# Tensor work of the attention units regrouped, four output buffers, a Sigmoid pass for the first gates, and a new order of the first stage

## The chip, the cores and the metric

One core of one Trainium2 chip runs the whole program. The metric is the device time of that core in microseconds. TensorE (PE) does the matrix products, VectorE (DVE), ScalarE (ACT) and GpSimd (POOL) work on its results, SyncE (SP) issues the transfers. All times of traces are counted from the start of the span of one profiled execution.

## The reference

Three parts follow each other. All data are float32.

```python
# linear attention with a gate, q, k, v, f_logit of shape (4, 8, 768, 48)
f = 1 / (1 + exp(-f_logit))
for t in range(S):
    state = f[t, :, None] * state + outer(k[t], v[t])     # 48 x 48 for each of 4 batches and 8 heads
    y[t] = q[t] @ state
# gated layer on 3072 tokens of width 384
xn = x / sqrt(mean(x * x) + 1e-6) * rms_g
x = (silu(xn @ w_gate) * (xn @ w_val)) @ w_out            # 384 -> 1536 -> 384
# second layer
out = relu(x @ w_in) ** 2 @ w_out2                        # 384 -> 2048 -> 384
```

## The kernel before, in words

The sequence of 768 is cut into 6 chunks of 128 steps. A *unit* is one chunk of one batch: 24 units in the order of chunks, units 0 to 3 being chunk 0. Four units are a *group* of 512 tokens, so there are six groups.

**A unit.** Two heads lie in each of four pairs, 64 partitions a head. The gate goes through `gate` (from unit 4 on, `sig` on both halves of `fr`: tanh, then an affine pass) or `gate_part` (units 0 to 3, `r` and `f` apart). VectorE runs a scan backwards (`scan_b`) and one forwards (`scan_a`), multiplies k and q by the results (`mul_k`, `mul_q`). TensorE then makes `scores` (L317, products of k and q of half height, two side by side), VectorE masks them (`mask_part`), TensorE transposes the keys (`ktrans`, L337) and ScalarE copies them out of PSUM (`kcopy`). `attend` (L352) adds two things in one PSUM bank: for chunks after the first the *inter-chunk products* q times state (L358, four, each 128 columns wide and 96 elements moving), and the *intra-chunk products* of masked scores and v (L371, sixteen, each 64 columns wide and 48 elements moving). `kv` (L378) makes the products of transposed keys and v that `state_add` adds to the state; the last chunk has neither `ktrans` nor `kv`. `norm`, `power`, `norm2` normalise the rows, `xtrans` transposes them, and `xhigh`, `xlow` split them into two fp32r parts (xh on ScalarE, L439, xl on VectorE, L446). Each of the float32 products is run by TensorE as two instructions, so four inter-chunk products are eight rows of the trace.

**The projections.** Every float32 weight and input is used as a high and a low part, and `mm3` makes three fp32r products of 512 (L555 to L557) for one. A step f of the gated layer has a piece G, a piece V and a piece O of nine such products each; between them stand Silu (si, L682), the product with V (vs, L687, on VectorE) and the split of the result (hh on ScalarE, L690, hl on VectorE, L692).

**The order of the first stage.** `first()` goes through the list `FIRST`, written out by hand. Every word is a piece and a number: l* are loads, gr and gf the gates, sb, sa, mk, mq, sc, ma, mb, kt, kc, y, kv, st, no, pw, nr, xt, xh, xl the parts of a unit in the order above (en keeps the last gate product, de decays the state), wl loads a pair of weights, ws, wb, wc make float32 of it, wh and wz split it, G, si, V, vs, hh, hl, O are a step of group 0. The list holds units 0 to 7, the 18 weight pairs of the gated layer and the twelve steps of group 0. Each engine takes its own pieces in this order and waits for what a piece needs. VectorE's pieces are sb, sa, mk, mq, ma, mb, xl, vs, hl, wb, wc, wz and st from unit 4 on.

**Phase 1.** For groups 1 to 5 `phase1` (L705) runs G, V and the O of the step before; behind each of the three stands a slot, and `plan_unit` (L582) puts the parts of units 8 to 23 into slots relative to the unit's own slot s, nine slots a unit. The slot's side parts (loads, ScalarE and VectorE) come ahead of the step's own ScalarE and VectorE work, its tail parts (TensorE) behind:

```python
(-9, (load_unit,)), (-3, (gate,)), (-2, (scan_b, keep_end)), (-1, (scan_a, mul_k)), (0, (mul_q, decay)),
(1, (masked,)), (2, (kcopy,)), (3, (norm, power)), (4, (state_add, norm2)), (6, (xhigh, xlow)),
...
((0, scores), (1, ktrans), (2, attend), (3, kv), (5, xtrans))
```

At a group's end `evac_x3` (L616) copies the three accumulators on ScalarE and stores them. The weights of the second layer are converted in phase 1 too.

**Phase 2.** For each group 16 steps: `project` (nine products of 512, written h), Relu on ScalarE (L751), square on VectorE (L752), split (L753, L754), and `seg_o2` (L729, twelve products of 384, written o) for the step before. At the last step of a group `seg_o2` copies four accumulators to SBUF, on ScalarE (L740) and VectorE (L738) in turn, into tiles of the tag qk, of which there are two, and stores each (L741). The next group's first `seg_o2` writes the same PSUM banks.

Of the kernel before, what the change touches and what calls it, by code (L numbers as in the profile page):

```python
# [8 lines left out]
F32 = mybir.dt.float32  # L9
# [3 lines left out]
AF = mybir.ActivationFunctionType  # L13
# [3 lines left out]
P = 128  # L17
B, H, S, D = 4, 8, 768, 48
# [3 lines left out]
DM = H * D  # L22
# [7 lines left out]


FIRST = """
lr0 lf0 lq0 lf1 lr1 gr0 lk0 lf3 gf0 sb0 sa0 mq0 lk1 lq1 gr1 lr2 lr3 gf1 mk0 lf2 sb1 sc0 gf3 lv0 wl0 mk1 gr2
mb0 kt0 sa1 kc0 lk2 gf2 lk3 mq1 sb2 lv1 sc1 lq2 lq3 kt1 ma0 kv0 en2 gr3 lv2 ma1 y0 ld4 mb1 st0 sa2 y1 kc1 no0
sb3 pw0 wl1 mk3 nr0 xt0 sa3 ws0 mq2 no1 lv3 ld5 mk2 xh0 pw1 nr1 wb0 sc2 kv1 xl0 xt1 st1 mq3 sc3 kt2 xh1 ma2
gr4 mb2 xl1 y2 mb3 ma3 ws1 wc0 sb4 y3 no2 kc2 wl2 no3 pw2 mk4 pw3 wb1 nr2 kv2 wh0 xt2 nr3 wc1 xt3 st2 sa4 wl3
xh3 xh2 mq4 wz0 sc4 wh1 xl3 ws2 xl2 kt3 G0 wz1 ws3 wb2 gr5 V0 wc2 wb3 wl4 kt4 si0 wc3 de4 G1 mb4 wh2 wl5 ma4
wh3 y4 wz2 ws4 vs0 wz3 kc4 wb4 hh0 kv4 V1 kc3 wc4 ws5 si1 hl0 kv3 no4 st4 G2 vs1 pw4 wb5 wl6 nr4 st3 xt4 wc5
O0 xh4 hh1 sb5 wl7 xl4 en5 V2 wh4 hl1 wh5 wz4 en4 si2 O1 ld6 wz5 ws6 vs2 ws7 wb6 G3 hh2 wc6 V3 hl2 wl8 wh6 wb7
wc7 si3 O2 mk5 wl9 wh7 gr6 wz6 wz7 G4 sa5 mq5 ws8 vs3 sb6 hh3 V4 si4 ws9 wb8 wc8 sc5 kt5 en0 G5 wb9 wh8 wl10  # L40
kc5 wz8 vs4 ma5 V5 hh4 hl3 hl4 wc9 si5 mk6 ws10 O3 de5 mb5 wl11 wh9 wb10 y5 en1 wc10 kv5 de6 wz9 wl12 O4 st5
ws11 kt6 vs5 G6 wb11 wh10 wz10 hh5 no5 wc11 ws12 V6 pw5 hl5 wl13 nr5 wb12 kc6 si6 xt5 O5 xh5 vs6 ld7 sa6 hh6
wh11 G7 xl5 hl6 wz11 mq6 V7 ws13 wc12 sc6 si7 wh12 wl14 wb13 gr7 wc13 O6 ma6 wl15 wz12 en3 G8 ws14 mb6 wh13
sb7 vs7 kv6 de7 y6 wz13 si8 wb14 hh7 hl7 ws15 G9 en6 wc14 wb15 O7 wh14 wl16 si9 wc15 wl17 no6 wh15 sa7 pw6 V8
nr6 wz15 xt6 mk7 G10 ld8 xh6 mq7 en7 st6 vs8 sc7 wz14 V9 hh8 xl6 ws16 ws17 mb7 ma7 hl8 y7 vs9 wb16 kt7 no7 O8
wc16 kc7 si10 pw7 wb17 hh9 V10 wh16 wc17 nr7 wz16 wh17 kv7 xt7 xh7 wz17 G11 vs10 xl7 V11 hl9 si11 st7 O9 hh10
vs11 hh11 hl10 O10 hl11 O11
"""


# [139 lines left out]
def tile_linear_attention_moe(  # L190
# [11 lines left out]
    nc = tc.nc  # L202
# [3 lines left out]
    def pool(name, **kw):  # L206
        return main.enter_context(tc.tile_pool(name=name, **kw))
# [6 lines left out]
    ap_ = pool("attn", bufs=2)  # L214
# [17 lines left out]
    state = [cp.tile([P, NPAIR, 2 * D], F32, name=f"state{b}") for b in range(B)]  # L232
# [21 lines left out]
    U = {}  # L254
# [23 lines left out]
    def sig(x):  # L278
        nc.scalar.activation(x, x, AF.Tanh, scale=0.5)
        nc.scalar.activation(x, x, AF.Identity, bias=half, scale=0.5)  # L280
# [2 lines left out]
        sig(U[u]["fr"].rearrange("p x a t -> p (x a) t")[:, :, 1:])  # L283

    def gate_part(n, u):
        sig(U[u][n][:, :, 1:])

    def scan_b(u):
        r = U[u]["r"]
# [24 lines left out]
    def banks(u):  # L314
        return ("pa", "pb", "pc") if u >= UG or u % 2 == 0 else ("acc0", "acc1", "acc2")
# [36 lines left out]
    def attend(u):  # L352
        c, b = units[u]
        y = ps.tile([P, DM], F32, tag=banks(u)[0], name=f"y{u}")
        first = True
        if c:
            for p in range(NPAIR):
                nc.tensor.matmul(  # L358
                    y[:, p * 2 * D:(p + 1) * 2 * D], U[u]["q"][:, p], state[b][:, p],
                    start=first, stop=False, skip_group_check=True,  # L360
                )
                first = False
        sub = [first, first]
        for hf in range(2):
            sm = U[u]["sm", hf]
            for j in range(4):
                h = 2 * j + hf
                hs = slice(h * D, (h + 1) * D)
                for i in range(2):
                    o = slice(64 * i, 64 * i + 64)  # L370
                    nc.tensor.matmul(  # L371
                        y[o, hs], sm[:, j, o], U[u]["v"][:, hs],
                        start=sub[i], stop=True, skip_group_check=True,
                    )
                    sub[i] = False
        U[u]["y"] = y
# [177 lines left out]
    def mm3(o, lh, ll, rh, rl, first, last):  # L554
        nc.tensor.matmul(o, lh, rh, start=first, stop=False)  # L555
        nc.tensor.matmul(o, lh, rl, start=False, stop=False)  # L556
        nc.tensor.matmul(o, ll, rh, start=False, stop=last)  # L557
# [21 lines left out]
    def at(where, s, fn):  # L579
        where.setdefault(max(s, NG), []).append(fn)  # L580

    def plan_unit(u, s):  # L582
        for k, fns in (
            (-9, (load_unit,)), (-3, (gate,)), (-2, (scan_b, keep_end)), (-1, (scan_a, mul_k)), (0, (mul_q, decay)),
            (1, (masked,)), (2, (kcopy,)), (3, (norm, power)), (4, (state_add, norm2)), (6, (xhigh, xlow)),
        ):
            for fn in fns:
                if fn is not load_unit or u > 2 * UG:
                    at(side, s + k, lambda fn=fn: fn(u))
        for k, fn in ((0, scores), (1, ktrans), (2, attend), (3, kv), (5, xtrans)):  # L590
            at(tail, s + k, lambda fn=fn: fn(u))

    NG = 3 * F1
    for gi in range(1, NU - 1):
        for j in range(UG):
            plan_unit((gi + 1) * UG + j, gi * NG + (3 if gi == 1 and j == 0 else (1, 10, 19, 28)[j]))
# [58 lines left out]
    def piece(kind, i):  # L655
        if kind in ("lr", "lk", "lf", "lq", "lv"):
            load_part(kind[1], i)
        elif kind in ("gr", "gf"):
            gate(i) if i >= UG else gate_part(kind[1], i)
        elif kind in ("ma", "mb"):  # L660
            mask_part(i, kind == "mb")
        elif kind in unit_piece:
            unit_piece[kind](i)
        elif kind in pair_piece:
            pair_piece[kind](w1_order[i])
        else:
            step_piece(kind, 0, i)

    unit_piece = dict(
        ld=load_unit, sb=scan_b, en=keep_end, sa=scan_a, mk=mul_k, mq=mul_q, sc=scores, kt=ktrans, kc=kcopy,  # L670
        y=attend, kv=kv, de=decay, st=state_add, no=norm, pw=power, nr=norm2, xt=xtrans, xh=xhigh, xl=xlow,
    )
    pair_piece = dict(wl=wload, ws=wscale, wb=wbits_low, wc=wbits_sign, wh=whigh, wz=wlow)
# [55 lines left out]
    def seg_o2(gi, f, hid, acc):  # L729
        wh, wl = W["b", f]  # L730
        for j in range(UG):
            cs = slice(j * C, (j + 1) * C)
            mm3(acc[j], hid[0][:, cs], hid[1][:, cs], wh, wl, f == 0, f == F2 - 1)
            if f == F2 - 1:
                c, b = units[gi * UG + j]
                o = ap_.tile([P, DM], F32, tag="qk", name=f"o_{gi}_{j}")
                if j % 2:
                    nc.vector.tensor_copy(o, acc[j])  # L738
                else:
                    nc.scalar.copy(o, acc[j])  # L740
                nc.sync.dma_start(out[b * S + c * C:b * S + (c + 1) * C, :], o)  # L741

    def phase2():
        for gi in range(NU):
            xh, xl = X[NU + gi]
            for f in range(F2):
                hps = ps.tile([P, N], F32, tag=("g", "vv")[f % 2], name=f"h2_{gi}_{f}")
                project(hps, ("a", f), xh, xl)
                sg = hp.tile([P, N], F32, tag="sg", name=f"r_{gi}_{f}")
                hh, hl = hidden(f"2_{gi}_{f}")  # L750
                nc.scalar.activation(sg, hps, AF.Relu)  # L751
                nc.vector.tensor_mul(sg, hps, sg)  # L752
                nc.scalar.copy(hh, sg)  # L753
                nc.vector.tensor_sub(hl, sg, hh.bitcast(F32))  # L754
                if gi + 1 < NU and f == 4:
                    load_x3(gi + 1)
                if gi + 1 < NU and f == 9:
                    parts.extend(split_x3(gi + 1))
                if parts:
                    parts.pop(0)()  # L760
                if pend:
                    pend.pop()()
                if f == 0:
                    acc = [ps.tile([P, DM], F32, tag=("acc0", "acc1", "acc2", "pa")[j], name=f"o2_{gi}_{j}") for j in range(UG)]
                pend.append(lambda gi=gi, f=f, hid=(hh, hl), acc=acc: seg_o2(gi, f, hid, acc))
        pend.pop()()
# [73 lines left out]
```

## Time and profile before

| | |
|---|---|
| median of 3 runs | 999.11 us (998.51 to 999.23) |
| the profiled execution, its own time | 998.11 us |
| its span | 996.3 us |
| mean granted clock of TensorE | 0.989 of full speed |
| TensorE busy | 967.3 us, 5757 products |
| VectorE busy | 506.6 us |
| ScalarE busy | 423.6 us |

How to read it: an engine's busy time is the time in which one of its instructions ran; products are pipelined, so a product's own duration (0.39 us for 512 columns) is longer than the distance to the next start. That distance is the cost. The granted clock is given as a share of 2.4 GHz; TensorE has a second level at 1.2 GHz, and a stretch with a mean between 0.5 and 1.0 has run at both. "Idle before, releaser" names what ended an idle time.

### The profile page before, as it was taken

The page shows a single profiled execution, that of the slowest core. Times are in us where ns is not written, and L with a number is a line of the kernel's source. Part 1 is how long each engine was busy: PE and PEld are TensorE (multiplying, and loading weights), DVE is VectorE, ACT ScalarE, POOL GpSimd, SP SyncE. Part 2 cuts the span into 40 slices and gives each one's busy share as a digit, 9 for nine tenths or more (in the row PEclk, how much of TensorE's full clock was granted, in tenths as well). Part 3 has the DMA queues.
Part 4 walks back from the last instruction along what each step waited for, and adds up shares of the span by engine and source line. Part 5 has one row for each costly group of instructions (what it writes and reads, how often), then busy time and mean ns, then how long its engine had stood idle before and what let it go on. Part 6 is the DMA issues. An engine that isn't in the chain of part 4 may idle for free.

```text
span 996.3 us, 14143 instructions
## 1 busy us (share of the span) xinstructions
PE 967.3 (97%) x5757; PEld 822.6 (83%) x5757; DVE 506.6 (51%) x777; ACT 423.6 (43%) x810; POOL 19.6 (2%) x42
## 2 busy tenths in 40 slices
PE   6799999999999999999999999999999999999996
PEld 4677878888888888888888889989989899899895
DVE  7999965555555666565522233333334334333332
ACT  6866645455455545454431233333323323333222
POOL 1000000000000000000000000000000000000000
PEclk7899999999999999999999999999999999999999
DMA  9455433334333433243036530010010100100001
GB/s 342 151 177 181 175 146 114 115 115 156 135 133 135 168 136 115 83 177 115 32 127 222 190 128 1 1 64 1 16 48 1 64 1 1 64 1 1 32 1 35
DMA packets 34744, 97.03 MB, mean 97 GB/s; under 512 B 4208, under 2 KB 10352, under 8 KB 34672
## 3 DMA queue, kind: packets, MB, share of 16 engines
q1 hardware_dynamic: 34672, 96.06, 27.3%
q8 instruction: 47, 0.77, 0.3%
q14 instruction: 25, 0.20, 0.1%
HBM read 74.02 MB, written 22.02 MB: 96 GB/s over the span
## 4 chain that ended last, share of the span: by engine, by line
PE 88%; DVE 6%; DMA 3%; ACT 1%; issue 1%; SPq 0%; DVEq 0%; ACTq 0%
PE o L555 7%; PE o L557 6%; PE h L556 6%; PE h L557 6%; PE o L556 6%; PE h L555 6%; PE acc L555 5%; PE v L555 5%; PE acc L557 5%; PE acc L556 5%; PE v L557 5%; PE v L556 5%; PE g L555 4%; PE g L557 4%; PE g L556 4%; PE y L371 2%
## 5 line engine op out<-in xcount | busy, mean ns | idle before, releaser
L752 DVE TENSOR_TENSOR r<-h,r 128x512 f32<-128x512 f32 x96 | 66.3, 691 | 181.9 <-ACT r L751 181.9
L751 ACT ACTIVATE r<-h 128x512 f32<-128x512 f32 x96 | 57.4, 598 | 190.1 <-PE h L557 190.1
L555 PE MATMUL o<-wh_a,hh 128*128 128x384 f32 x384 | 130.0, 339 | 0.6
L557 PE MATMUL o<-wh_a,hl 128*128 128x384 f32 x384 | 129.7, 338 | 0.1
L556 PE MATMUL o<-wl_a,hh 128*128 128x384 f32 x384 | 129.0, 336 | 0.0
L557 PE MATMUL h<-xh,wl_a 128*128 128x512 f32 x288 | 113.9, 396 | 0.0
L556 PE MATMUL h<-xl,wh_a 128*128 128x512 f32 x288 | 113.7, 395 | 0.0
L555 PE MATMUL h<-xh,wh_a 128*128 128x512 f32 x288 | 112.0, 389 | 0.0
L687 DVE TENSOR_TENSOR sg<-v,sg 128x512 f32<-128x512 f32 x72 | 49.7, 690 | 119.7 <-PE v L557 117.5
L754 DVE TENSOR_TENSOR hl<-r,hh 128x512 fp32r<-128x512 f32 x96 | 66.4, 692 | 65.9 <-PE o L557 56.9
L753 ACT CAST hh<-r 128x512 fp32r<-128x512 f32 x96 | 59.6, 621 | 74.2 <-DVE r L752 74.2
L682 ACT ACTIVATE sg<-g 128x512 f32<-128x512 f32 x72 | 43.0, 597 | 110.1 <-PE g L557 107.8
L690 ACT CAST hh<-sg 128x512 fp32r<-128x512 f32 x72 | 44.4, 616 | 89.9 <-DVE sg L687 87.3
L555 PEld LDWEIGHTS o<-wh_a,hh 128*128 128x128 f32 x384 | 72.1, 188 | 7.0 <-DVE o L738 2.2
L556 PEld LDWEIGHTS o<-wl_a,hh 128*128 128x128 f32 x384 | 72.1, 188 | 4.1
L557 PEld LDWEIGHTS o<-wh_a,hl 128*128 128x128 f32 x384 | 72.0, 188 | 0.4 <-DVE hl L754 0.4
L557 PEld LDWEIGHTS h<-xh,wl_a 128*128 128x128 f32 x288 | 54.0, 187 | 11.6
L556 PEld LDWEIGHTS h<-xl,wh_a 128*128 128x128 f32 x288 | 54.0, 187 | 9.1
L555 PEld LDWEIGHTS h<-xh,wh_a 128*128 128x128 f32 x288 | 54.1, 188 | 8.7
L692 DVE TENSOR_TENSOR hl<-sg,hh 128x512 fp32r<-128x512 f32 x72 | 49.0, 682 | 14.3 <-ACT hh L690 13.7
L555 PE MATMUL v<-xh,wh_g 128*128 128x512 f32 x108 | 44.1, 408 | 1.5 <-DVE sg L687 1.5
L555 PE MATMUL v<-xh,wh_v 128*128 128x512 f32 x108 | 44.2, 409 | 0.7 <-DVE sg L687 0.7
(127 smaller groups left out, 1832.1 us busy)
## 6 DMA issues: line engine op xcount, KB each, us to landing
raw<-in_w_dram SPq DMA_DIRECT2D x34, 768.0 KB, 4.4
w2d<-ws_a SPq DMA_DIRECT2D x32, 384.0 KB, 2.5
ff<-in_ff_dram SPq DMA_DIRECT2D x20, 516.0 KB, 4.6
qk<-in_qk_dram SPq DMA_DIRECT2D x20, 512.0 KB, 5.7
wh_a<-w2d SPq DMA_DIRECT2D x16, 384.0 KB, 3.1
wl_a<-w2d SPq DMA_DIRECT2D x16, 384.0 KB, 3.9
v<-in_vp_dram SPq DMA_DIRECT2D x24, 192.0 KB, 5.7
x3d<-x3o SPq DMA_DIRECT2D x18, 256.0 KB, 2.1
```

Source lines behind the costliest of these rows:

```text
L371: nc.tensor.matmul(y[o, hs], sm[:, j, o], U[u]["v"][:, hs], start=sub[i], stop=True, skip_group_check=True,)
L555: nc.tensor.matmul(o, lh, rh, start=first, stop=False)
L556: nc.tensor.matmul(o, lh, rl, start=False, stop=False)
L557: nc.tensor.matmul(o, ll, rh, start=False, stop=last)
L682: nc.scalar.activation(dd["s", f], dd["g", f], AF.Silu)
L687: nc.vector.tensor_mul(dd["s", f], dd["v", f], dd["s", f])
L690: nc.scalar.copy(dd["h", f][0], dd["s", f])
L692: nc.vector.tensor_sub(dd["h", f][1], dd["s", f], dd["h", f][0].bitcast(F32))
L751: nc.scalar.activation(sg, hps, AF.Relu)
L752: nc.vector.tensor_mul(sg, hps, sg)
L753: nc.scalar.copy(hh, sg)
L754: nc.vector.tensor_sub(hl, sg, hh.bitcast(F32))
```

## The change

1. `attend`: each inter-chunk product is made in two of 64 columns, in the two halves of the array, in turn.
2. `plan_unit`: the key transposes move from slot 1 to slot 0, ahead of the scores; their copy from slot 2 to slot 1; k v moves from slot 3 to slot 2, behind the intra-chunk products.
3. `seg_o2`: the copies of accumulators 2 and 3 go to tiles of the tag ff, so a group has four output buffers.
4. `gate_part`: one Sigmoid pass for r and f of units 0 to 3, where tanh and an affine pass stood.
5. `FIRST`: the same 385 pieces in another order.

```diff
--- before.py
+++ after.py
@@ -30,21 +30,21 @@
 
 
 FIRST = """
-lr0 lf0 lq0 lf1 lr1 gr0 lk0 lf3 gf0 sb0 sa0 mq0 lk1 lq1 gr1 lr2 lr3 gf1 mk0 lf2 sb1 sc0 gf3 lv0 wl0 mk1 gr2
-mb0 kt0 sa1 kc0 lk2 gf2 lk3 mq1 sb2 lv1 sc1 lq2 lq3 kt1 ma0 kv0 en2 gr3 lv2 ma1 y0 ld4 mb1 st0 sa2 y1 kc1 no0
-sb3 pw0 wl1 mk3 nr0 xt0 sa3 ws0 mq2 no1 lv3 ld5 mk2 xh0 pw1 nr1 wb0 sc2 kv1 xl0 xt1 st1 mq3 sc3 kt2 xh1 ma2
-gr4 mb2 xl1 y2 mb3 ma3 ws1 wc0 sb4 y3 no2 kc2 wl2 no3 pw2 mk4 pw3 wb1 nr2 kv2 wh0 xt2 nr3 wc1 xt3 st2 sa4 wl3
-xh3 xh2 mq4 wz0 sc4 wh1 xl3 ws2 xl2 kt3 G0 wz1 ws3 wb2 gr5 V0 wc2 wb3 wl4 kt4 si0 wc3 de4 G1 mb4 wh2 wl5 ma4
-wh3 y4 wz2 ws4 vs0 wz3 kc4 wb4 hh0 kv4 V1 kc3 wc4 ws5 si1 hl0 kv3 no4 st4 G2 vs1 pw4 wb5 wl6 nr4 st3 xt4 wc5
-O0 xh4 hh1 sb5 wl7 xl4 en5 V2 wh4 hl1 wh5 wz4 en4 si2 O1 ld6 wz5 ws6 vs2 ws7 wb6 G3 hh2 wc6 V3 hl2 wl8 wh6 wb7
-wc7 si3 O2 mk5 wl9 wh7 gr6 wz6 wz7 G4 sa5 mq5 ws8 vs3 sb6 hh3 V4 si4 ws9 wb8 wc8 sc5 kt5 en0 G5 wb9 wh8 wl10
-kc5 wz8 vs4 ma5 V5 hh4 hl3 hl4 wc9 si5 mk6 ws10 O3 de5 mb5 wl11 wh9 wb10 y5 en1 wc10 kv5 de6 wz9 wl12 O4 st5
-ws11 kt6 vs5 G6 wb11 wh10 wz10 hh5 no5 wc11 ws12 V6 pw5 hl5 wl13 nr5 wb12 kc6 si6 xt5 O5 xh5 vs6 ld7 sa6 hh6
-wh11 G7 xl5 hl6 wz11 mq6 V7 ws13 wc12 sc6 si7 wh12 wl14 wb13 gr7 wc13 O6 ma6 wl15 wz12 en3 G8 ws14 mb6 wh13
-sb7 vs7 kv6 de7 y6 wz13 si8 wb14 hh7 hl7 ws15 G9 en6 wc14 wb15 O7 wh14 wl16 si9 wc15 wl17 no6 wh15 sa7 pw6 V8
-nr6 wz15 xt6 mk7 G10 ld8 xh6 mq7 en7 st6 vs8 sc7 wz14 V9 hh8 xl6 ws16 ws17 mb7 ma7 hl8 y7 vs9 wb16 kt7 no7 O8
-wc16 kc7 si10 pw7 wb17 hh9 V10 wh16 wc17 nr7 wz16 wh17 kv7 xt7 xh7 wz17 G11 vs10 xl7 V11 hl9 si11 st7 O9 hh10
-vs11 hh11 hl10 O10 hl11 O11
+lr0 lf0 lk0 lq0 lr1 gr0 sb0 lf1 lk1 gf0 wl0 mk0 gr1 sa0 gf1 mq0 kt0 lv0 lr2 sb1 sc0 lq1 mk1 lr3 ws0 ma0 lf2
+sa1 lk3 gr2 lv1 mb0 lq2 wb0 lf3 kc0 lk2 kt1 mq1 kv0 st0 lq3 wc0 gf2 ld4 sb2 kc1 sc1 sa2 mq2 gr3 wh0 y0 no0 pw0
+wl1 gf3 mb1 kv1 ma1 mk2 y1 st1 lv2 nr0 lv3 wz0 ld5 no1 pw1 xt0 sc2 sb3 mk3 sa3 mq3 xh0 nr1 xt1 sc3 gr4 wl2 xl0
+kt2 mb2 ma2 ma3 y2 ws1 xh1 kc2 mb3 y3 wb1 kv2 no2 pw2 no3 pw3 en3 xl1 nr2 xt2 sb4 sa4 mk4 nr3 xt3 st2 xh3 mq4
+wc1 wl3 xh2 sc4 ws2 xl3 xl2 kt3 wb2 ma4 kc3 G0 wh1 de4 en1 V0 wz1 en4 wc2 ws3 kt4 mb4 si0 G1 wb3 wh2 vs0 wz2
+kv3 en2 wl4 wc3 gr5 sb5 ws4 wl5 V1 kc4 kv4 wh3 wb4 wc4 wl6 y4 si1 hh0 wz3 G2 wh4 no4 pw4 vs1 V2 mk5 hh1 wz4
+ws5 hl1 st3 ld6 hl0 wb5 wc5 ws6 kt5 kc5 nr4 wb6 O0 si2 vs2 wl7 O1 wc6 sa5 hh2 xt4 wh5 en0 G3 wl8 xh4 mq5 wh6
+wz5 ws7 xl4 V3 si3 wz6 st4 sc5 ws8 wb7 vs3 wc7 wl9 hh3 G4 V4 wb8 wh7 gr6 hl2 O2 wc8 hl3 si4 ma5 O3 wl10 wh8
+wz7 wz8 vs4 ws9 wb9 hh4 ws10 mb5 de5 G5 wc9 wh9 en5 y5 wb10 wc10 wl11 wl12 si5 V5 wz9 hl4 wh10 vs5 no5 pw5
+ws11 wz10 G6 wb11 kv5 ld7 nr5 hh5 xt5 xh5 O4 hl5 O5 wc11 si6 xl5 wl13 ws12 sb6 en6 de6 mk6 kt6 st5 wh11 gr7 V6
+G7 si7 kc6 wb12 wc12 wl14 sa6 mq6 vs6 wz11 sb7 wh12 sc6 hh6 V7 ws13 wz12 G8 hl6 O6 wb13 ws14 vs7 hh7 V8 si8
+wc13 wl15 mb6 de7 ma6 hl7 wb14 wc14 wh13 wh14 y6 no6 wl16 O7 sa7 wz13 pw6 kv6 vs8 mq7 hh8 st6 ws15 G9 mk7 nr6
+wz14 kt7 sc7 wb15 kc7 si9 xt6 ws16 V9 wc15 wl17 hl8 O8 xh6 wh15 xl6 wz15 vs9 wb16 hh9 hl9 G10 V10 ws17 wc16
+wh16 mb7 si10 wb17 O9 ma7 y7 wc17 wh17 en7 wz16 G11 vs10 wz17 hh10 hl10 no7 V11 ld8 pw7 si11 vs11 kv7 st7 nr7
+xt7 O10 hh11 hl11 O11 xh7 xl7
 """
 
 
@@ -283,7 +283,8 @@
         sig(U[u]["fr"].rearrange("p x a t -> p (x a) t")[:, :, 1:])
 
     def gate_part(n, u):
-        sig(U[u][n][:, :, 1:])
+        x = U[u][n][:, :, 1:]
+        nc.scalar.activation(x, x, AF.Sigmoid)
 
     def scan_b(u):
         r = U[u]["r"]
@@ -352,15 +353,16 @@
     def attend(u):
         c, b = units[u]
         y = ps.tile([P, DM], F32, tag=banks(u)[0], name=f"y{u}")
-        first = True
+        sub = [True, True]
         if c:
             for p in range(NPAIR):
-                nc.tensor.matmul(
-                    y[:, p * 2 * D:(p + 1) * 2 * D], U[u]["q"][:, p], state[b][:, p],
-                    start=first, stop=False, skip_group_check=True,
-                )
-                first = False
-        sub = [first, first]
+                for i in range(2):
+                    o = slice(64 * i, 64 * i + 64)
+                    nc.tensor.matmul(
+                        y[o, p * 2 * D:(p + 1) * 2 * D], U[u]["q"][:, p, o], state[b][:, p],
+                        start=sub[i], stop=False, skip_group_check=True,
+                    )
+                    sub[i] = False
         for hf in range(2):
             sm = U[u]["sm", hf]
             for j in range(4):
@@ -582,12 +584,12 @@
     def plan_unit(u, s):
         for k, fns in (
             (-9, (load_unit,)), (-3, (gate,)), (-2, (scan_b, keep_end)), (-1, (scan_a, mul_k)), (0, (mul_q, decay)),
-            (1, (masked,)), (2, (kcopy,)), (3, (norm, power)), (4, (state_add, norm2)), (6, (xhigh, xlow)),
+            (1, (kcopy, masked)), (3, (norm, power)), (4, (state_add, norm2)), (6, (xhigh, xlow)),
         ):
             for fn in fns:
                 if fn is not load_unit or u > 2 * UG:
                     at(side, s + k, lambda fn=fn: fn(u))
-        for k, fn in ((0, scores), (1, ktrans), (2, attend), (3, kv), (5, xtrans)):
+        for k, fn in ((0, ktrans), (0, scores), (2, attend), (2, kv), (5, xtrans)):
             at(tail, s + k, lambda fn=fn: fn(u))
 
     NG = 3 * F1
@@ -733,7 +735,7 @@
             mm3(acc[j], hid[0][:, cs], hid[1][:, cs], wh, wl, f == 0, f == F2 - 1)
             if f == F2 - 1:
                 c, b = units[gi * UG + j]
-                o = ap_.tile([P, DM], F32, tag="qk", name=f"o_{gi}_{j}")
+                o = ap_.tile([P, DM], F32, tag=("qk", "ff")[j // 2], name=f"o_{gi}_{j}")
                 if j % 2:
                     nc.vector.tensor_copy(o, acc[j])
                 else:
```

## Rows read from the trace of the kernel before

**Rows 1.** The page: span, and busy time of each engine.

```profile
span 996.3 us, 14143 instructions
...
PE 967.3 (97%) x5757; PEld 822.6 (83%) x5757; DVE 506.6 (51%) x777; ACT 423.6 (43%) x810; POOL 19.6 (2%) x42
```

**Rows 2.** Stretches: length; busy and instructions of PE, PEld, DVE, ACT, POOL; clock; DMA.

```profile
6.50:79.00 72.50, 56.76 (x509) 46.22 (x509) 70.03 (x106) 54.34 (x107) 3.97 (x5) 0.88 0.62 221
146.00:500.00 354.00, 353.87 (x2398) 289.54 (x2397) 208.56 (x329) 171.91 (x356) 8.76 (x16) 1.00 0.34 122
```

**Rows 3.** Timeline of PE around one unit: start, duration, instruction.

```profile
191.59 0.48 PE L555 MATMUL g<-xh,wh_o 128*128 128x512 f32 x1
191.91 0.39 PE L556 MATMUL g<-xl,wh_o 128*128 128x512 f32 x1
...
193.50 0.39 PE L557 MATMUL g<-xh,wl_o 128*128 128x512 f32 x1
193.73 1.02 PE L358 MATMUL y<-state,qk 128*128 128x96 f32 x8
194.69 1.14 PE L371 MATMUL y<-v,sm 128*64 128x48 f32 x32
...
196.09 0.40 PE L556 MATMUL v<-xl,wh_v 128*128 128x512 f32 x1
...
197.71 0.40 PE L557 MATMUL v<-xh,wl_v 128*128 128x512 f32 x1
198.04 0.56 PE L386 MATMUL kv<-v,ktok 128*48 128x48 f32 x16
...
198.87 0.40 PE L556 MATMUL acc<-hl,wh_o 128*128 128x512 f32 x1
```

**Rows 4.** Timeline of PE, unit 5 of the first stage.

```profile
83.04 0.39 PE L557 MATMUL acc<-hh,wl_v 128*128 128x512 f32 x1
...
85.19 0.53 PE L386 MATMUL kv<-v,ktok 128*48 128x48 f32 x16
...
85.99 0.40 PE L556 MATMUL acc<-hl,wh_o 128*128 128x512 f32 x1
```

**Rows 5.** Timeline of PEld (weight loads), the same unit as rows 3.

```profile
187.96 0.97 PEld L323 LDWEIGHTS sc<-qk 64*128 64x128 f32 x16 [0.35 <-issue]
...
194.68 1.01 PEld L371 LDWEIGHTS y<-v,sm 128*64 128x64 f32 x32
```

**Rows 6.** Waits: who waited for whom, us in total, times, longest.

```profile
ACT o L740 <- DMA out_dram<-o: 13.2, 6, 3.3
...
PEld o L555 <- DVE o L738: 2.2, 5, 0.5
```

**Rows 7.** Timeline of all engines, the end of phase 2.

```profile
986.89 0.34 PE L557 MATMUL o<-wh_a,hl 128*128 128x384 f32 x1
...
989.92 0.56 DVE L738 COPY o<-o 128x384 f32<-128x384 f32 x1 [3.14 <-DMA out_dram<-o]
```

**Rows 8.** The chain that ended last, the end of phase 2: start, us, what.

```profile
986.80 3.00 DMA out_dram<-o
```

**Rows 9.** Timeline of the first stage and the start of phase 1.

```profile
0.81 1.28 ACT L279 ACT_TABLE_LOAD   x1 [0.81 <-PEq L829]
...
5.70 0.72 ACT L280 ACTIVATE r<-r,half 128x512 f32<-128x512 f32 x1
...
6.52 1.23 DVE L290 TENSOR_TENSOR_SCAN r<-r,floor 128x516 f32<-128x516 f32 x1 [6.52 <-ACT r L280]
...
79.09 0.47 PE L555 MATMUL v<-xh,wh_v 128*128 128x512 f32 x1 [0.72 <-DVE sg L687]
...
135.76 1.95 ACT L619 COPY x3o<-acc 128x512 f32<-128x512 f32 x3 [2.10 <-PE acc L557]
...
144.94 1.16 PE L323 MATMUL sc<-qk 64*128 64x128 f32 x16 [1.74 <-DVE qk L304]
```

**Rows 10.** Groups by line: busy us, mean ns of one, idle before.

```profile
L439 ACT ACTIVATE xh<-xtp,gT 128x128 fp32r<-128x128 f32 x72 | 20.9, 368 | 2.8 <-PE xtp L428 2.7
```

## The prediction

> **What bounds the kernel now.** I read the page first: TensorE is busy for 967 of 996.3 us, VectorE for half of that [rows 1]. So two questions decide: what fills TensorE, and where its 29 us of idle lie. The view by stretches answers the second. From 6.5 to 79 us VectorE is the bound: busy 70.03 of 72.5 us, while TensorE idles 15.7 us, at a granted clock of 0.88, so part of it at the lower level, 1.2 GHz [rows 2]. From 146 to 500 us TensorE is busy 353.87 of 354 us and VectorE 208.56 [rows 2]. There every microsecond taken off TensorE comes off the end. The last idle stretch is the end of phase 2, after the last product.
>
> The timeline of TensorE around one unit (unit 10, 188 to 199 us) shows what a unit costs beside the projections. Seven projection products lie between 191.91 and 193.50 us, 0.227 us each [rows 3]. After the key transposes the first product takes 0.32 us to the next start (191.59 to 191.91), 0.09 too long. The attention visit runs from the start of the product ahead of it (193.50) to the second one behind it (196.09): 2.59 us, of it 0.96 (193.73 to 194.69) the eight instructions of the inter-chunk products, including the change to the half-width ones. The k v visit, measured in the same way, is 1.16 us (197.71 to 198.87), with 0.33 from the product ahead to its own start instead of 0.227: changing to half-width products and back costs time each time.
>
> **k v behind the intra-chunk products.** Two separate visits take 2.59 + 1.16 us and contain two ordinary steps more than a joint one: 3.75 - 2 x 0.227 = 3.30 us. In the first stage there is a joint one already, from 83.04 to 85.99 us, 2.95 us [rows 4]. Gain 0.35 us less reading error: I take 0.34 for each of units 8 to 19 (the last chunk has no k v): 12 x 0.34 = **4.1 us**. Nothing takes its place: the copy of the transposed keys still has one whole step of nine products and the next projection between the transposes and k v; if ScalarE were late by more than that, TensorE would wait at k v for it.
>
> **Key transposes ahead of the scores.** The separate visit ends in the 0.09 us of above; joined to the scores, that end falls together with the change that the scores cost anyway. 0.09 for eleven units: **1.0 us** (unit 8 stands in a wait, below). Bounds 0 and 0.2 each.
>
> **Inter-chunk products split.** Eight full-width instructions become sixteen of 64 columns, moving 96 elements. No row shows this shape. Bounds: the half-width products of the intra-chunk part move 48 elements at 1.01/32 = 31.6 ns of weight loads each; the scores, two half-arrays side by side, move 128 at 0.97/16 = 60.6 ns [rows 5]. In proportion to what moves, 96 of 128 gives 45 ns, 0.73 us for sixteen; the change to half width (0.10) now stands ahead of them and not behind. 0.73 + 0.10 against 0.96: gain 0.13. The ends: 16 x 31.6 ns would gain 0.35, 16 x 60.6 ns would lose 0.11. I take 0.13, since the scores are nearest in size: 16 units x 0.13 = **2.1 us** (-1.8 to +5.6). Against it speaks the Trainium skill, "TensorEngine Tiling (Array Packing)", section Instruction Overhead: about 60 cycles for each matmul, so tiling doesn't pay from a dimension that is already small. By it eight more instructions would cost some 0.2 us a unit, an estimate from that page, and the sum would be 5 us higher; no row here shows that price, and the 31.6 ns products bear it out only in part.
>
> **Four output buffers.** In phase 2 the third and fourth copy of each group wait for a transfer: ScalarE 13.2 us in six waits [rows 6]. TensorE feels it at the five inner group borders, where a weight load waits 2.2 us in total for the last copy [rows 6]. With a buffer for each copy these end: **2.0 us**. At the end the last product starts at 986.89 and runs 0.34 us, but the last copy starts only at 989.92 [rows 7]; it could start at 987.27, 2.65 us earlier. A transfer there takes 3.00 us with two in flight [rows 8]. With four in flight the gain lies between 0.7 (the second pair moves wholly behind the first: lands at 992.8 and not at 993.5) and 2.65. I take **2.2 us**, nearer to the second end, since the two transfers of that row are in flight together and still take no longer than 3.00.
>
> **The first stage.** VectorE starts at 6.52 us, when ScalarE has done tanh and a 0.72 us affine pass on the first gate [rows 9]. One Sigmoid pass drops the 0.72, and seven more behind it: VectorE starts 0.7 earlier. A table load takes 1.28 us on ScalarE [rows 9], and the program has two; a third one by this change would cost between 0 and 1.28; I take 0, since it would fall where VectorE has queued work. The Trainium skill, "ScalarE: Activation LUTs", section Table sets: the hidden batching unit, lists tanh in sigmoid's set, so by it none is added; no row here shows Sigmoid. VectorE's idle of 72.5 - 70.03 = 2.5 us to 79 us is mostly waiting for ScalarE early on; I take 0.5 back. The same pieces stand in both written orders, so VectorE's total is fixed and only places move. The piece that decided before is V5, the last one for which TensorE waited, at 79.09 us, for the gated product of step 4 [rows 9]. I count 105 VectorE instructions in the order up to that product (the window up to 79 us has 106 [rows 2], 0.66 us each); the new order has 103, and one O piece and one unit's attention fewer behind it. G8 comes next: 136 instructions instead of 139 ahead of its weights, but fourteen steps of nine products instead of thirteen behind: about -2 and +2 us. So I give the order 0.3. Weight load wl0 now stands ahead of the second unit's loads on SP's queue and delays them; sb1 and the weights' work are there to cover it, else VectorE idles, see the rivals.
>
> One step is worse: xh7 and xl7 now stand behind O11. ScalarE's three copies after O11 ran from 135.76 for 1.95 us [rows 9]; behind them comes xh7 (368 ns a piece [rows 10]), then xl7, about as long (an estimate from that row), ahead of the first G of group 1: TensorE idles some 1.3 us. But 1.74 us of waiting for unit 8's scores (at 144.94 us [rows 9]) follow anyway. Unit 8's gate is put back by three pieces of xh7, some 0.9 us, and the transposes now fill 0.4 of that wait: net +0.4. First stage: -0.7 - 0.5 - 0.3 + 0.4 = **-1.1 us**.
>
> **Sum:** 4.1 + 1.0 + 2.1 + 2.0 + 2.2 + 1.1 = 12.5 us. The profiled execution took 998.11 us, so 985.6; the median shown is 999.11, 1.0 above it. Forecast 986.6 us.
>
> **Rivals.**
> 1. *The split costs time.* At 60.6 ns or more per half-width product the term is -1.8 instead of +2.1: 990.5 us. For it: twice the instructions. Against it: 31.6 ns for the existing half-width ones. The skill page above is this rival's rule; by its price the time would be 991.9, an estimate. Chance 0.13.
> 2. *The first stage slips.* The late loads of units 1 to 3, a third table load and the wait for xl7 add up on VectorE's start of the dense part: 4 to 5 us more, 991. For it: only 2.5 us of VectorE idle to win back, more to lose. Chance 0.17.
> 3. *VectorE runs dry ahead of G0: slower.* The new order does the weights of V0 behind 23 VectorE instructions, before behind 46: the work that filled the waits for four units' normalisation is spent early. Each microsecond that VectorE then idles comes at the end one for one, and TensorE, idling too, starts the dense part at 1.2 GHz. It decides from 10.5 us of extra idle (no change) and is slower from 14.5. Price with 15 us: 1001.6. Against it: ScalarE has 5.8 us less to do there. Chance 0.10 (0.04 within 0.2%, 0.06 beyond).
> 4. *The first stage gains more:* all 2.5 us of VectorE idle return: 984.5. Chance 0.05.
> That the joint visits don't come about is no rival of its own: the order of the slots fixes them; only the first stage's own k v pieces stay apart for units 5 to 7.
>
> **Numbers.** Forecast 0.55. Range: from 980.5 (the better first stage with the split at 31.6 ns, 3.5 us better, less a little) to 993 (rivals 1 and 2 half joined, or the last pair of transfers at its bad end). A measurement of this kernel can tell 0.2%, 2 us, from no change. Faster: all but rival 3, 0.90; same 0.04; slower 0.06.
>
> **What would show it.** In the profile after: the unit visit in TensorE's timeline with k v right behind the intra-chunk products, without a visit of its own, and sixteen inter-chunk instructions in 0.7 to 0.8 us. A unit of chunks 2 to 4 then takes 0.56 us less from its scores to the next unit's. No wait of ScalarE or VectorE copies for the output transfer. VectorE's first scan at 5.8 us. An idle of TensorE of about 1.3 us ahead of the first G of group 1. It is wrong if VectorE shows more than 5 us of idle up to 79 us, if TensorE waits for transposed keys at k v, or if the sixteen instructions take over 0.96 us.

## The result, and the profile after

The changed kernel takes 983.81 us (median of four, 983.71 to 984.16), the kernel before in the same session 998.81: a ratio of 0.9852, 95% interval 0.9835 to 0.9869. Forecast were 986.6 us and a gain of 12.5; the gain is 15.0 us by the medians and 14.3 by the two profiled spans. The numbers of the source lines moved by one to three: L358 is L361 now, L371 L373, L555 to L557 are L557 to L559.

The page of the changed kernel, span and busy time [rows 1]:

```profile
span 982.0 us, 14472 instructions
...
PE 959.8 (98%) x5917; PEld 818.6 (83%) x5917; DVE 506.6 (52%) x777; ACT 417.4 (43%) x802; POOL 17.8 (2%) x42
```

TensorE has 160 products more (twenty units with eight instructions more each) and is busy 7.5 us less; VectorE's work is the same to a tenth; ScalarE, without the eight affine passes, is busy 6.2 us less. The stretches, in the same columns and between the same times as [rows 2] (VectorE now starts at 5.44 us, ahead of the first):

```profile
6.50:79.00 72.50, 62.36 (x553) 50.76 (x554) 70.40 (x108) 52.17 (x106) 3.19 (x5) 0.84 0.62 225
...
146.00:500.00 354.00, 354.00 (x2563) 291.59 (x2563) 212.12 (x335) 173.74 (x362) 9.22 (x16) 1.00 0.35 124
```

VectorE still bounds the first and TensorE the second. Up to 79 us TensorE now idles 10.1 us and not 15.7, but at a granted clock of 0.84 and not 0.88, so part of the longer busy time is work at the lower level. VectorE has done 108 instructions and not 106.

TensorE's timeline of unit 10, the same unit as [rows 3] (start, duration, instruction):

```profile
185.38 0.39 PE L559 MATMUL v<-xh,wl_g 128*128 128x512 f32 x1
185.60 0.60 PE L343 MATMUL ktp<-ident,qk 128*128 128x128 f32 x4
186.13 1.16 PE L324 MATMUL sc<-qk 64*128 64x128 f32 x16
187.22 0.50 PE L557 MATMUL acc<-hh,wh_v 128*128 128x512 f32 x1
...
191.22 0.39 PE L559 MATMUL g<-xh,wl_o 128*128 128x512 f32 x1
191.53 0.88 PE L361 MATMUL y<-state,qk 128*64 128x96 f32 x16
192.24 1.09 PE L373 MATMUL y<-v,sm 128*64 128x48 f32 x32
193.16 0.53 PE L388 MATMUL kv<-v,ktok 128*48 128x48 f32 x16
193.62 0.50 PE L557 MATMUL v<-xh,wh_v 128*128 128x512 f32 x1
193.96 0.39 PE L558 MATMUL v<-xl,wh_v 128*128 128x512 f32 x1
...
208.93 1.16 PE L324 MATMUL sc<-qk 64*128 64x128 f32 x16
```

The scores of units 10 and 11 in the kernel before, for the distance between them:

```profile
187.96 1.16 PE L323 MATMUL sc<-qk 64*128 64x128 f32 x16
...
211.39 1.16 PE L323 MATMUL sc<-qk 64*128 64x128 f32 x16
```

The sixteen half-width inter-chunk instructions take 0.71 us (191.53 to 192.24), 44 ns each, where eight full-width ones took 0.96; the change of width now stands ahead of them (0.31 from 191.22, 0.08 more than a step). The intra-chunk products take 0.92 and not 1.06, for they begin and end without a change. k v follows at once, 0.46 us. The distance from one unit's scores to the next is 22.80 us in chunks 2 to 4 (here 186.13 to 208.93), where it was 23.43 (187.96 to 211.39).

The end of phase 2 and the first stage, from the timelines (compare [rows 7] and [rows 9]):

```profile
5.44 1.23 DVE L291 TENSOR_TENSOR_SCAN r<-r,floor 128x516 f32<-128x516 f32 x1 [5.44 <-ACT r L287]
...
134.36 0.39 PE L559 MATMUL acc<-hh,wl_v 128*128 128x512 f32 x1
135.69 0.50 PE L557 MATMUL g<-xh,wh_g 128*128 128x512 f32 x1 [0.94 <-ACT xh L441]
136.60 0.50 PE L558 MATMUL g<-xl,wh_g 128*128 128x512 f32 x1 [0.40 <-DVE xl L448]
...
143.32 0.66 PE L343 MATMUL ktp<-ident,qk 128*128 128x128 f32 x4 [0.54 <-DVE qk L302]
144.61 1.16 PE L324 MATMUL sc<-qk 64*128 64x128 f32 x16 [0.64 <-DVE qk L305]
...
975.48 0.34 PE L559 MATMUL o<-wh_a,hl 128*128 128x384 f32 x1
...
975.86 0.56 DVE L740 COPY o<-o 128x384 f32<-128x384 f32 x1 [0.49 <-PE o L559]
```

The last copy starts 0.38 us after the start of the last product, where it was 3.03 [rows 7]. No copy waits for the output transfer any more. O11's last product starts at 134.36 (before at 136.70), but TensorE then stops for xh7 (0.94 us), xl7 (0.40), unit 8's keys (0.54) and unit 8's queries (0.64).

Where the 14.3 us came from, by marks in the two timelines (us from the span's start; each difference is the part's own length):

| stretch | before | after | difference |
|---|---|---|---|
| start to unit 8's scores | 144.94 | 144.61 | -0.33 |
| unit 8's scores to unit 23's | 343.97 | 335.10 | -8.87 |
| unit 23's scores to the last product | 497.98 | 495.77 | -2.21 |
| last product to the end of the span | 9.41 | 6.52 | -2.89 |

### The profile page after: what moved, and what is told of

Same layout as the page of the kernel before. It is cut to its first block, busy times and chain, and to the rows that moved or that the text cites. A ratio compares the mean times of both kernels' runs of the same rounds, so it can differ in the third digit from the quotient of the medians.

```text
span 982.0 us, 14472 instructions
## 1 busy us (share of the span) xinstructions
PE 959.8 (98%) x5917; PEld 818.6 (83%) x5917; DVE 506.6 (52%) x777; ACT 417.4 (43%) x802; POOL 17.8 (2%) x42
## 4 chain that ended last, share of the span: by engine, by line
PE 90%; DVE 6%; ACT 1%; issue 1%; DMA 0%; POOL 0%; SPq 0%; DVEq 0%; ACTq 0%
PE h L558 7%; PE o L559 7%; PE h L559 7%; PE o L557 7%; PE o L558 7%; PE h L557 7%; PE acc L557 5%; PE v L557 5%; PE acc L559 5%; PE acc L558 5%; PE v L559 5%; PE v L558 5%; PE g L557 4%; PE g L558 4%; PE g L559 4%; PE sc L324 3%
## 5 line engine op out<-in xcount | busy, mean ns | idle before, releaser
L559 PE MATMUL o<-wh_a,hl 128*128 128x384 f32 x384 | 129.7, 338 | 0.1
L557 PE MATMUL o<-wh_a,hh 128*128 128x384 f32 x384 | 129.4, 337 | 0.0
L559 PE MATMUL h<-xh,wl_a 128*128 128x512 f32 x288 | 113.9, 396 | 0.0
L557 PE MATMUL h<-xh,wh_a 128*128 128x512 f32 x288 | 111.9, 389 | 0.0
L689 DVE TENSOR_TENSOR sg<-v,sg 128x512 f32<-128x512 f32 x72 | 49.7, 691 | 117.0 <-PE v L559 112.4
L557 PEld LDWEIGHTS o<-wh_a,hh 128*128 128x128 f32 x384 | 72.2, 188 | 4.6 <-ACT hh L755 0.3
L559 PEld LDWEIGHTS o<-wh_a,hl 128*128 128x128 f32 x384 | 72.0, 188 | 0.4 <-DVE hl L756 0.4
L559 PEld LDWEIGHTS h<-xh,wl_a 128*128 128x128 f32 x288 | 54.0, 187 | 11.5
L557 PEld LDWEIGHTS h<-xh,wh_a 128*128 128x128 f32 x288 | 54.1, 188 | 8.6
L557 PE MATMUL v<-xh,wh_v 128*128 128x512 f32 x108 | 44.2, 409 | 0.0
L557 PE MATMUL g<-xh,wh_g 128*128 128x512 f32 x108 | 43.2, 400 | 0.9 <-ACT xh L441 0.9
```

The costliest lines, as they stand in the source:

```text
L689: nc.vector.tensor_mul(dd["s", f], dd["v", f], dd["s", f])
```

## The experiments

Each kernel below is the changed kernel with one thing altered, compared with 983.81 us. The diffs are against the changed kernel. All times are medians of four executions, with the lowest and highest; the kernel before stood at 998.4 to 998.7 beside them. Four executions of one kernel spread by up to 1.6 us, so where a difference is 1 us or so, the reading rests on marks in the traces, one execution of each kernel.

**Inter-chunk products at full width again.**

```diff
-                for i in range(2):
-                    o = slice(64 * i, 64 * i + 64)
-                    nc.tensor.matmul(
-                        y[o, p * 2 * D:(p + 1) * 2 * D], U[u]["q"][:, p, o], state[b][:, p],
+                nc.tensor.matmul(
+                    y[:, p * 2 * D:(p + 1) * 2 * D], U[u]["q"][:, p], state[b][:, p],
```

> The changed kernel with the inter-chunk products at full width again. My theory: the split saves 0.16 us in its own sixteen instructions (0.80 with the change of width ahead of them, 0.96 before) and 0.06 because the intra-chunk products no longer begin with a change of width; the last units' period says 0.22 together. So 16 x 0.22 = 3.5 us in phase 1, up to 0.9 more from units 4 to 7: 987.3 to 988.2 us, and the distance of two units' scores in chunk 5 back from 22.00 to 22.22 us. Rival: the split itself is worth nothing and the last units gain from the smaller number of visits: under 1 us, 983.8 to 984.8.

988.07 us (987.67 to 988.27), ratio to the kernel before 0.9887 (0.987 to 0.9903). The scores' distance is 22.22 us in chunk 5 and 23.02 in chunks 2 to 4: 0.22 a unit in both. The timeline of unit 10 in this kernel:

```profile
192.40 1.02 PE L359 MATMUL y<-state,qk 128*128 128x96 f32 x8
193.36 1.14 PE L372 MATMUL y<-v,sm 128*64 128x48 f32 x32
194.33 0.53 PE L387 MATMUL kv<-v,ktok 128*48 128x48 f32 x16
```

The inter-chunk part takes 0.96 us, the intra-chunk part 0.97, in the changed kernel 0.71 + 0.08 and 0.92. Unit 8's scores come 0.51 us later; counted from VectorE's start they come after 139.64 us, and in four kernels that have the same first stage (the changed one and the runs with old slots, with the old transposes and with two buffers) after 139.17 to 139.51. So a gain of units 4 to 7 from the split is not shown. In phase 1 the split is worth what the theory says, and the rival falls.

**The halves one after the other.**

```diff
-            for p in range(NPAIR):
-                for i in range(2):
+            for i in range(2):
+                for p in range(NPAIR):
```

> The changed kernel with the eight half-width inter-chunk instructions of the first half all ahead of those of the second, same work. Theory: the split pays because the two halves of the array work side by side, so that 44 ns an instruction is half of what one takes; one half alone then needs 80 ns or more each, 16 x 36 = 0.6 us more a unit, over 9 us in phase 1: 993 us or more. Rival: it pays because each weight load is half as wide; then the order of the halves makes no difference, 983.8 us within 1.

990.93 us (990.88 to 991.02): 7.1 more. Both theories missed the size. The scores' distance is 23.19 us, 0.39 a unit and not 0.6. TensorE's timeline of unit 10 in this kernel shows why:

```profile
193.22 1.01 PE L361 MATMUL y<-state,qk 128*64 128x96 f32 x13
193.99 0.26 PE L373 MATMUL y<-v,sm 128*64 128x48 f32 x1
194.07 0.25 PE L361 MATMUL y<-state,qk 128*64 128x96 f32 x1
194.09 0.22 PE L373 MATMUL y<-v,sm 128*64 128x48 f32 x1
...
194.24 0.25 PE L361 MATMUL y<-state,qk 128*64 128x96 f32 x1
194.25 0.97 PE L373 MATMUL y<-v,sm 128*64 128x48 f32 x26
```

Sixteen instructions start over 1.03 us, 64 ns each where in turn they need 44. The first intra-chunk instructions start between the last three inter-chunk ones, so part of the lost time is won back there. In this order the split is dearer than the full width: the distance of 23.19 us stands against 23.02. So the gain hangs on the halves taking turns, and the narrower weight load alone doesn't bring it. That two instructions then run side by side in the two halves fits this, but is inferred.

**Key transposes, their copy and k v in the old slots.**

```diff
-            (1, (kcopy, masked)), (3, (norm, power)), ...
+            (1, (masked,)), (2, (kcopy,)), (3, (norm, power)), ...
-        for k, fn in ((0, ktrans), (0, scores), (2, attend), (2, kv), (5, xtrans)):
+        for k, fn in ((0, scores), (1, ktrans), (2, attend), (3, kv), (5, xtrans)):
```

> The changed kernel with key transposes, their copy and k v in their old slots. Theory: the distance of two units' scores in chunks 2 to 4 grows from 22.80 to 23.21 us, that of chunk 5 stays at 22.00; twelve units at 0.41 us: 988.7 us. The prediction's prices would make it 12 x 0.34 + 11 x 0.09 = 5.1 us, 988.9. Rival: most of the gain of phase 1 is the split's, and the visits' places are worth under 2 us: under 985.8.

990.52 us (989.51 to 990.96). The distance is 23.18 us, 0.38 a unit, and 22.00 in chunk 5. From unit 8's scores to unit 23's it is 340.38 us, 5.3 more than in the changed kernel. The profiled span is 5.7 longer, the median 6.7; the profiled execution was the fastest of four that spread by 1.45 us, and the microsecond between is not explained.

**Only the key transposes and their copy in the old slots.** The same edit, with k v left at slot 2.

> The changed kernel with the key transposes and their copy in their old slots, k v still behind the intra-chunk products. Theory: of the 0.41 us a unit, k v's visit has 0.34 and the transposes' 0.07 to 0.09: 984.7 to 984.9 us, scores to scores 22.88 us. Rival: the two share the gain about evenly: 986.2.

985.01 us (984.99 to 985.26). The total fits, the reason doesn't: the distance is 22.82 us, only 0.02 more than in the changed kernel. So k v's place is worth 23.18 - 22.82 = 0.36 a unit and the transposes' 0.02. The timeline of unit 10 in this kernel shows the separate visits:

```profile
186.54 0.39 PE L559 MATMUL v<-xh,wl_g 128*128 128x512 f32 x1
186.85 1.16 PE L324 MATMUL sc<-qk 64*128 64x128 f32 x16
187.95 0.50 PE L557 MATMUL acc<-hh,wh_v 128*128 128x512 f32 x1
...
190.13 0.60 PE L343 MATMUL ktp<-ident,qk 128*128 128x128 f32 x4
190.48 0.48 PE L557 MATMUL g<-xh,wh_o 128*128 128x512 f32 x1
```

Ahead of a projection the four transposes take 0.35 us; ahead of the scores, in the changed kernel, 0.53 (185.60 to 186.13). What the joint visit saves, 0.09 behind the transposes and 0.08 ahead of the scores (186.54 to 186.85 is 0.31), it pays between the two. Most of the 1.2 us lies at unit 8: its transposes no longer fill a wait (0.46: to unit 9's scores it is 19.18 us and not 18.72), and 0.3 of waiting comes back ahead of unit 9's scores.

**Two output buffers.**

```diff
-                o = ap_.tile([P, DM], F32, tag=("qk", "ff")[j // 2], name=f"o_{gi}_{j}")
+                o = ap_.tile([P, DM], F32, tag="qk", name=f"o_{gi}_{j}")
```

> The changed kernel with two output buffers. Theory: five group borders at 0.41 us and 2.9 us between the last product and the end of the span: 4.9 us, 988.7 us; waits of ScalarE and VectorE copies for the output transfer return at 13 us each. Rival: the borders cost nothing on TensorE, only the end does: 2.9 us, 986.7.

988.93 us (988.01 to 989.65): 5.1 more. The view of waits of this kernel shows the three waits again:

```profile
DVE o L740 <- DMA out_dram<-o: 13.0, 6, 3.0
ACT o L742 <- DMA out_dram<-o: 13.0, 6, 3.1
PEld o L557 <- DVE o L740: 2.2, 5, 0.5
```

Its last product starts at 977.30, 1.82 later than in the changed kernel, although unit 8's scores were 0.16 earlier: 1.98 for the five borders. From there to the end of the span it is 9.0 us instead of 6.5. The borders' cost is the theory's, and the rival falls. The end is less sharp: 6.5 is the lowest of nine kernels with four buffers, which take up to 7.06.

**The old order of the first stage.** `FIRST` as before, Sigmoid kept.

> The changed kernel with the order of the first stage from before. Theory of the prediction: the new order is worth some 0.3 us ahead of O11 and costs 0.4 behind it, so no more than 1 us either way: 983 to 985 us. What I now read from the trace: O11 ends 2.3 us earlier than before, but 2.0 of it are lost at the wait for xl7 and for unit 8; with the old order and the Sigmoid pass O11 ends some 1.3 us later than in the changed kernel, and the tail costs 1.7 us less: 983.0 to 984.0. Rival: the new order is what brings O11 forward, the Sigmoid pass does nothing: 2 us or more slower, 985.8 or more.

983.39 us (983.12 to 984.44), 0.4 less than the changed kernel, with overlapping times: no gain of the new order as a whole is seen. The marks of its first stage, VectorE's start and O11's last product:

```profile
4.94 1.23 DVE L291 TENSOR_TENSOR_SCAN r<-r,floor 128x516 f32<-128x516 f32 x1 [4.94 <-ACT r L287]
...
135.13 0.39 PE L559 MATMUL acc<-hh,wl_v 128*128 128x512 f32 x1
```

From VectorE's start to O11 it is 130.19 us, with the kernel before 136.70 - 6.52 = 130.18. So in this order, by these two profiles, only VectorE's start moves the end of the stage. In the changed kernel it is 128.92, and 129.10 to 129.26 in the three other kernels with the same first stage: the new order saves 0.9 to 1.3 there, and gives it back behind O11, where it is 10.25 us to unit 8's scores and in this run 8.25.

**Tanh and the affine pass again.**

```diff
-        x = U[u][n][:, :, 1:]
-        nc.scalar.activation(x, x, AF.Sigmoid)
+        sig(U[u][n][:, :, 1:])
```

> The changed kernel with tanh and the affine pass for the first eight gates. Theory: VectorE starts 0.7 us later and ScalarE has 5.8 us more ahead of G0; VectorE is the bound there, so the end comes 0.7 to 1.5 us later: 984.5 to 985.3. Rival: the waits behind O11 (unit 8, xl7) take it up, no change within 0.4 us.

985.00 us (984.21 to 985.67): 1.2 more, within the theory's bounds. VectorE starts at 5.78 and O11's last product at 134.63, 128.85 apart as in the changed kernel (128.92): no gain up to O11 is seen from the 5.8 us that ScalarE is spared ahead of G0. VectorE starts 1.54 us after ScalarE's first pass, in the changed kernel 0.73, so the Sigmoid pass is worth 0.81 at the start. By the profile the start differs only by 0.34, since the first gate's transfer landed 0.47 earlier in this execution (the first pass starts at 4.24, in the changed kernel at 4.71). That the start makes up the 1.2 us is not shown: the profiled spans differ by 1.0, of which 0.27 stands at O11, 0.2 falls in the middle of phase 1 and 0.5 behind the last product.

**xh7 and xl7 ahead of O10.**

```diff
-xt7 O10 hh11 hl11 O11 xh7 xl7
+xt7 xh7 xl7 O10 hh11 hl11 O11
```

> The changed kernel with xh7 and xl7 ahead of O10 and not behind O11. Theory: TensorE's waits for them ahead of the first G of group 1 (0.9 and 0.4 us in the trace, 1.9 us by the starts of the products) go; unit 8's gate moves forward by 0.8 us with them, so its scores wait for VectorE about 1 us less in time, and the end comes about 0.8 to 1.3 us earlier: 982.5 to 983.0. Rival: the wait moves whole to unit 8's scores, which hang on ScalarE's copies behind O11 and not on xh7: no change, 983.8 within 0.4.

982.84 us (982.46 to 983.29), 1.0 less, as the theory said; by the profiles, counted from VectorE's start, unit 8's scores come 1.27 earlier (137.90 us and not 139.17). The wait ahead of the first G is gone, but those for unit 8 have not changed by a hundredth:

```profile
141.58 0.66 PE L343 MATMUL ktp<-ident,qk 128*128 128x128 f32 x4 [0.54 <-DVE qk L302]
142.88 1.16 PE L324 MATMUL sc<-qk 64*128 64x128 f32 x16 [0.64 <-DVE qk L305]
```

So they don't hang on xh7. What they hang on stands in VectorE's rows, first in the changed kernel, then in this one:

```profile
138.32 1.23 DVE L291 TENSOR_TENSOR_SCAN ff<-ff,floor 128x516 f32<-128x516 f32 x1 [1.26 <-ACT ff L280]
...
140.85 0.69 DVE L689 TENSOR_TENSOR sg<-v,sg 128x512 f32<-128x512 f32 x1 [1.08 <-PE v L559]
141.46 1.22 DVE L299 TENSOR_TENSOR_SCAN ff<-ff,seed 128x516 f32<-128x516 f32 x1
```

```profile
137.73 1.23 DVE L291 TENSOR_TENSOR_SCAN ff<-ff,floor 128x516 f32<-128x516 f32 x1 [4.97 <-ACT ff L280]
139.00 0.18 DVE L292 RECIPROCAL seed<-ff 128x4 f32<-128x4 f32 x1
139.11 0.69 DVE L689 TENSOR_TENSOR sg<-v,sg 128x512 f32<-128x512 f32 x1
139.72 1.22 DVE L299 TENSOR_TENSOR_SCAN ff<-ff,seed 128x516 f32<-128x516 f32 x1
```

Unit 8's forward scan (L299) stands behind the product with V of step 0 of group 1 (L689). In the changed kernel that product waits for TensorE: the whole row moves with it. In this run V's last product (138.62, 0.39 us long) and the backward scan with its reciprocal end within 0.2 us of each other, and that scan waited for unit 8's gate, which ScalarE makes directly behind its three copies. So the rival's time is wrong, but the copies hold the row here about as much as TensorE does, and this run doesn't separate the two.

**Unit 8's gate, scans and products moved into the first stage as well.** Its parts leave `plan_unit`.

```diff
-G11 ... V11 ld8 pw7 si11 vs11 kv7 st7 nr7
-xt7 O10 hh11 hl11 O11 xh7 xl7
+G11 ... V11 ld8 pw7 gr8 si11 sb8 vs11 kv7 st7 nr7
+xt7 xh7 xl7 O10 hh11 hl11 en8 sa8 mk8 mq8 O11
```

> The changed kernel with xh7 and xl7 ahead of O10 as before, and unit 8's gate, scans and products with k and q moved from the first slots of phase 1 into the last part of the first stage, where ScalarE and VectorE idle. Theory: what is left there, waits of 0.54 us for unit 8's keys and 0.64 for its queries, hangs on VectorE's row of that work behind the product with V of step 0; ahead of O11 it costs nothing, so the waits go: 1.2 us less than with xh7 and xl7 moved alone, 981.6 us. Rival: the gate delays si11 and with it O11, and half of it is given back: 982.3.

981.35 us (981.02 to 982.19), ratio to the kernel before 0.9824 (0.9808 to 0.9841), 1.5 less than the run above. Both possible causes are gone in it, the scans behind the product and the gate behind the copies, and its timeline has no wait at the two places:

```profile
141.42 0.60 PE L343 MATMUL ktp<-ident,qk 128*128 128x128 f32 x4
141.95 1.16 PE L324 MATMUL sc<-qk 64*128 64x128 f32 x16
```

This version beats both kernels, the changed one by 2.5 us.

## Why the prediction was right, and where its terms were off

The forecast held because the stage that holds most of the change was read rightly: from unit 8's scores on TensorE is the bound without a gap, and the places where visits cost time could be measured in the kernel before. Term by term:

- **k v behind the intra-chunk products**, 4.1 forecast: 0.36 a unit by the runs, 12 x 0.36 = 4.3. The joint visit of [rows 4] was the right row to go by.
- **Key transposes ahead of the scores**, 1.0 forecast: 0.02 a unit, 0.2. The step that failed is "that end falls together with the change that the scores cost anyway": a change of 0.53 - 0.35 = 0.18 us comes in between transposes and scores instead. The lower bound, 0, was the better choice.
- **Inter-chunk products split**, 2.1 forecast: 16 x 0.22 = 3.5. The pace was met (45 ns forecast, 44 measured). The term missed that the intra-chunk products, too, lose the change of width ahead of them: 0.16 a unit is the split's own and 0.06 theirs. Rival 1 is out: in turn, sixteen instructions cost less than eight. With the halves one after the other, 23.19 us against 23.02, it would have been right; the prediction never made the turns a condition. By the rule that it cites for this rival from the Trainium skill, "TensorEngine Tiling (Array Packing)", section Instruction Overhead, eight more instructions would have cost some 0.2 us a unit, an estimate; the trace doesn't agree, 0.71 us for the sixteen against 0.96 for the eight.
- **Four output buffers**, 2.0 and 2.2 forecast: 2.0 at the borders. At the end the last copy comes 2.65 us earlier behind the last product, the upper bound (2.46 against the run with two buffers). From the last product to the end of the span it is 9.41 and 9.00 us with two buffers and 6.52 to 7.06 in nine kernels with four: 1.9 to 2.9, with the changed kernel's profile at the best end. The two pairs of transfers did overlap: from the last copy to the end it is 6.14 to 6.68 us with four buffers, 6.16 and 6.38 with two.
- **The first stage**, 1.1 forecast: 0.33 at unit 8's scores, and 0.46 for the transposes that already stand ahead of them, so 0.8. The sum hides two errors. VectorE's start was given 0.7 and moved by 1.08, of which 0.27 is the landing of the first transfer and 0.81 the Sigmoid pass; no third table load came, ScalarE has two before and after, so the 0 taken for it held. The order and VectorE's idle were given 0.8 ahead of O11 and brought 0.9 to 1.3. The tail was given a net loss of 0.4; from O11's last product to unit 8's scores it grew from 8.24 to 10.25 us, 2.0, less the 0.46 for the transposes 1.55. The idle itself was read rightly, 1.3 forecast and 0.94 + 0.40 measured. The step that failed is that unit 8's wait would take it up: unit 8's forward scan stands on VectorE behind a product that waits for TensorE (1.08 us in the changed kernel), so the wait moves along. With xh7 and xl7 moved ahead of O10 it is 8.34 us again.

Rival 2 had the right place, the wait for xl7, but about a quarter of its size; rival 3 did not come: VectorE idles 2.1 of 72.5 us up to 79 us, by the stretch above. The parts of a unit add up to 0.60 of the 0.63 us by which the distance fell; 0.03 stays unassigned.

Some of the closeness is luck. The transposes and the first stage together brought 1.1 us less than forecast, and the split 1.4 more. The split's sign, too, was open: its bounds ran from -1.8 to +5.6, and no row of the kernel before showed its shape.

## What to carry to other kernels

Where TensorE is the bound, count the changes of array shape in a unit of work and put products of one shape next to each other; but check the shape on both sides, since here transposes joined to half-height products saved 0.02 us only. A full-width product like these (128 columns, 96 elements moving, float32) can gain by a split into two halves if the halves take turns (44 ns an instruction); one after the other (64 ns) it lost. A wait that is expected to swallow another one must hang on something that does not move with it: follow the releaser's own queue before letting one idle absorb the next.

## What the runs showed that was not expected

The landing of the first gate's transfer varied between executions: ScalarE's first pass starts at 4.98 us in the profile of before, at 4.71 after and at 4.24 with tanh. VectorE bounds what follows, but such a difference passes on to O11 in part only: with two buffers VectorE starts 0.50 earlier than in the changed kernel and O11's last product 0.16. So comparisons of the first stage in single profiles are good to about half a microsecond, and to 0.3 when they are made from VectorE's start.

The old order also shows a stop in the middle of phase 1 that the changed kernel lacks, at one unit's masks (timeline of TensorE, run with the old order):

```profile
327.82 0.62 PE L373 MATMUL y<-v,sm 128*64 128x48 f32 x16
328.87 0.67 PE L373 MATMUL y<-v,sm 128*64 128x48 f32 x16 [0.42 <-DVE sm L331]
```

That distance of two scores is 23.43 us instead of 22.80, so half of the 1.2 us by which this run was ahead at unit 8 is lost there (0.5 of the 1.2 was its earlier start). The masks' tiles share their tag with the group's stored copies, and in the changed kernel VectorE's masks wait 6.9 us in two places for that store without a stop of TensorE. Here the longer of these waits ends with the store's landing after 4.5 us, where it was 3.9; the three stores took 3.5 us to landing in the median and not 3.0. Why they were slower is open. Smaller stops stand at the same place in the run with tanh (23.00) and in the last run (22.95).
